# Attention into two mixtures on one core: 64-row score products, division after the value product, and first-mixture weight parts kept in DRAM

## The chip, the cores and the metric

One core of a Trainium2 chip runs the whole program. The metric is the device time of one execution in microseconds (us), the median of three runs for the kernel before. The profile is of one further execution. Engines are named as in the profile: PE (TensorE matmul), PEld (TensorE weight load), DVE (VectorE), ACT (ScalarE), POOL (GpSimd), SP (SyncE, which issues nearly all transfers).

## What is computed

```python
scores = scale * np.matmul(q, k.transpose(0, 1, 3, 2))     # 4 batches, 12 heads, 448 tokens, 64 wide
scores = np.where(mask, -1000000000.0, scores)             # causal
attn = np.exp(scores - np.max(scores, axis=-1, keepdims=True))
attn = attn / (np.sum(attn, axis=-1, keepdims=True) + 1e-09)
x = np.matmul(attn, v)                                     # then 1792 tokens x 768
h = np.maximum(np.maximum(x @ w1, x @ w2), x @ w3)         # first mixture, 768 x 768 each
y = h @ w_out
# second mixture: one of 8 experts per token, 768 -> 1024 -> 768, scaled by its gates
```

w1, w2, w3 and w_out arrive as 64-bit floats and are decoded on the chip; the rest is 32-bit.

## The kernel before, in words

The work goes in four batches of 448 tokens. A **unit** u is one pair of heads of one batch: units 0 to 5 are batch 0, 6 to 11 batch 1, up to 23. The two heads of a unit sit in partitions 0 to 63 and 64 to 127.

**First stage** (`first_heads`, an order written out by hand): attention of units 0 to 5, and the decoding of w_out and of three of the 18 chunks of w1 to w3. A chunk is 128 columns of one of the three matrices; the code cuts each matrix into six. The three chunks go to `wdram`.

**Middle stages** (`batch(b)`, b = 0, 1, 2; `mix`): `h_stream(b)` makes the hidden layer of batch b, chunk by chunk, and beside it the generator `attn_stream` computes the attention of batch b + 1, at 0.95 steps for each step of the host stream; `y_half` then multiplies by w_out for three or four blocks of 128 tokens, again with attention steps beside it. The order on each engine comes from a planner that sorts by priority; `ahead` runs with a higher one. **Batch 3** of `h_stream` runs without attention, beside the first loads of expert weights (`first_load`, 14 transfers). The second mixture follows, slot by slot.

Numbers on PE are carried as a high and a low part (float32r): a product is made of two or three matmuls. The steps around the change, per unit:

- `at_t` (L223): PE transposes q and k into PSUM. For units 0 to 9 (`NATQ`) they are copied as plain float32; from unit 10 on q and k are split: `qs` holds for each head the high part in its 64 partitions and the low part in the other 64, `ks` holds k's high part in both halves (written by L250 and copied across by L253), `kl` k's low part (L251).
- `at_qk` (L256): the scores of a head and of a block i of 112 queries against 112(i + 1) keys, so 112 to 448 columns. Units 0 to 9: one float32 product over 64 rows (L274). From unit 10: one product over 128 rows, high times high and low times high at once (L276), and one over 64 rows for k's low part (L278).
- `at_e` (L282): DVE adds the mask and finds the maximum (L292), ACT makes the exponential and the row sum (L297).
- `at_n` (L304): from unit 6 on, DVE adds 1e-9 to the sums (L308), takes the reciprocal (L309) and multiplies the four blocks of each head's probabilities by it (L315). For units 0 to 5 the probabilities are left as they are; `at_rb` and `at_r` spread the reciprocal over 64 columns (ACT, L320), transpose it (four PE transposes, L327) and copy it out (ACT), and `at_x` multiplies each head's finished value product by it (DVE, L398).
- `at_p` (L336): PE transposes the probabilities (L350), ACT and DVE split them (L361, L362). `at_av` (L365): the product with v; ACT moves the other half of the result across (L391) and DVE adds it into `xf` (L392).
- `x_split` (L450) splits `xf` for `h_stream`, once a unit is done.

The scores, transposes and value products share six PSUM banks (`ps_t`). From unit 12 on and in the first stage both heads' scores are made at once (six banks); for units 6 to 11 one head at a time (`at_s`).

The weights of the first mixture: `w_fetch` (L466) brings a chunk into `wr`. In batch 0 it is decoded from two raw halves (`decode_load` on SP, two ACT, three DVE and one POOL instruction each, L143 to L155) and written to `wdram` (L472); in batches 1 to 3 it is read back from there (L474). `w_split` (L477) then makes the high part on ACT (L482) and the low part on POOL (L483), in every batch. `ahead` keeps chunks fetched three to four ahead of use and split one to two ahead. SP issues in one order, so a fetch that waits for a free buffer holds back what is queued behind it.

```python
for a, (l, r) in enumerate(((wh, xh), (wh, xl), (wl, xh))):   # L515, six times a chunk
    nc.tensor.matmul(pm[:, :S], lhsT=l[:, kk, :], rhs=r, ...)
```

Of the kernel before, what the change touches and what calls it, by code (L numbers as in the profile page):

```python
# [32 lines left out]
def kernel(  # L33
# [221 lines left out]
    def at_qk(u, js):  # L255

        qs, ks, kl = qks[u]
        for i in range(NC):
# [3 lines left out]
            for j in js:  # L262
                m = M[j]
# [7 lines left out]
                sl.append((j, m, ss))  # L271
            for j, m, ss in sl:
                if u in NATQ:
                    nc.tensor.matmul(ss, lhsT=qs[m, 0, qc], rhs=ks[m, 0, :L], start=True, stop=True)  # L274
# [25 lines left out]
    def at_s(u, j, beside=()):  # L300
        at_qk(u, (j,))
        at_e(u, j, beside)

    def at_n(u, j):  # L304
        if u in NATP and j == 0:
            return
        sm = sums[u] if u in NATP else sums[u][:, j]
        nc.vector.tensor_scalar_add(sm, sm, 1e-9)  # L308
        nc.vector.reciprocal(sm, sm)  # L309
        if u in NATP:  # L310
            return
# [5 lines left out]
    def at_rb(u):  # L317
        rb = att.tile([P, 512], F32, tag="mn", name=f"rb{u}", bufs=1)[:CP].rearrange("p (c j d) -> p c j d", c=NC, j=2)
        sb = sums[u].rearrange("p j c -> p c j").unsqueeze(3).to_broadcast([CP, NC, 2, D])
        nc.scalar.copy(rb, sb)  # L320
# [851 lines left out]
```

## Time and profile before

| | |
|---|---|
| three runs | 1019.55, 1024.61, 1024.18 us; median 1024.18 |
| the profiled execution | 1027.47 us, span on the core 1025.8 us |
| PE, PEld busy in the span | 94%, 81% |
| DVE, ACT, POOL busy | 61%, 52%, 29% |
| mean granted clock of PE | 0.965 of full |
| moved by DMA | 122.95 MB, 120 GB/s in the mean |
| chain of waits, by engine | PE 65%, DVE 22%, ACT 5%, DMA 3% |

Times inside the profile are counted from the start of the span. The first matmul of `h_stream` starts at 99.4 us and its batches 1 to 3 at 287.1, 439.9 and 583.5; `y_half` of batch 2 ends at 594, `h_stream(3)` alone runs from there to 652.4, and the second mixture's slots run from about 704 to the end. Ends of matmuls are modelled, so a matmul's own row is longer than the time from its start to the next one's start.

### The profile page before, as it was taken

To read this page: it belongs to the slowest core of one execution; us is meant where nothing else is said; L and a number is where in the kernel's file an instruction comes from. 1 tells how busy PE (TensorE), PEld (TensorE's weight loads), DVE (VectorE), ACT (ScalarE), POOL (GpSimd) and SP (SyncE) were. 2 spreads that over 40 slices of the span, in tenths; PEclk is the share of its full clock that TensorE was granted. 3 is DMA by queue.
4 is the path that set the end of the run, shared out by engine and by line. 5 is a ranking of instruction groups with operands and counts; after the bars stand their busy time and mean duration, and the time that the engine had idled before them with its cause. 6 is when DMAs were issued, how large, how long until landed. Compare 5 with 4: busy or idle time off the path is not lost.

```text
span 1025.8 us, 16765 instructions
## 1 busy us (share of the span) xinstructions
PE 965.5 (94%) x5188; PEld 833.4 (81%) x5188; DVE 629.5 (61%) x1504; ACT 528.7 (52%) x1181; POOL 302.5 (29%) x249
## 2 busy tenths in 40 slices
PE   7998898888999999999998999988999999999997
PEld 4676676676887888897887989977989989898896
DVE  5887888999587877657788542292111114939344
ACT  7887564666565666545766223251212124838243
POOL 2445644544022335122444155132010100010101
PEclk9998987899998999998999999999999999999999
DMA  7566554642222333223312185036010112949600
GB/s 166 147 163 182 171 156 148 181 134 77 63 66 74 101 93 89 82 66 88 89 63 62 48 279 183 24 109 239 35 63 32 38 57 88 358 159 353 212 31 25
DMA packets 116418, 122.95 MB, mean 120 GB/s; under 512 B 74830, under 2 KB 92238, under 8 KB 116304
## 3 DMA queue, kind: packets, MB, share of 16 engines
q1 hardware_dynamic: 113264, 108.24, 34.1%
q0 software_dynamic: 3040, 13.41, 3.8%
q8 instruction: 44, 0.72, 0.3%
q14 instruction: 70, 0.57, 0.2%
HBM read 109.80 MB, written 19.69 MB: 126 GB/s over the span
## 4 chain that ended last, share of the span: by engine, by line
PE 65%; DVE 22%; ACT 5%; DMA 3%; issue 3%; SPq 1%; POOL 1%; DVEq 0%; POOLq 0%; ACTq 0%
PE pm L516 16%; PE po L1068 14%; PE ph L1049 14%; PE py L548 8%; DVE pt L315 5%; PE ss L276 2%; DVE ptl L362 2%; PE pp L350 2%; PE av L386 2%; PE ss L278 2%; ACT pt L297 2%; DMA xg<-ydram,gix 2%; DVE pt L292 2%; DVE dt L152 2%; PE pht L1060 1%
## 5 line engine op out<-in xcount | busy, mean ns | idle before, releaser
L483 POOL TENSOR_TENSOR wl<-wr,wh 128x768 fp32r<-128x768 f32 x72 | 134.6, 1869 | 206.5 <-ACT wh L482 186.6
L516 PE MATMUL pm<-xh,wh 128*128 128x448 f32 x432 | 169.7, 393 | 0.0
L516 PE MATMUL pm<-xh,wl 128*128 128x448 f32 x432 | 162.1, 375 | 1.0 <-POOL wl L483 1.0
L516 PE MATMUL pm<-xl,wh 128*128 128x448 f32 x432 | 162.3, 376 | 0.3 <-POOL xl L454 0.3
L297 ACT ACTIVATE pt<-pt,bm 112x112 f32<-112x112 f32 x192 | 100.7, 526 | 69.3 <-DVE bm L292 66.1
L1063 DVE TENSOR_TENSOR tl<-pht,th 128x512 fp32r<-128x512 f32 x36 | 24.8, 688 | 136.1 <-ACT th L1062 86.0
L1077 POOL DMA_INDIRECT out_dram<-os,six x18 | 18.4, 1020 | 283.5 <-ACT os L1076 171.4
L1068 PE MATMUL po<-w2h,th 128*128 128x384 f32 x288 | 100.7, 350 | 0.0
L1068 PE MATMUL po<-w2h,tl 128*128 128x384 f32 x288 | 97.6, 339 | 1.8 <-DVEq L1098 1.8
L1068 PE MATMUL po<-w2l,th 128*128 128x384 f32 x288 | 97.7, 339 | 0.0
L292 DVE CUSTOM_DVE_ANT_0 pt<-ss,mask 112x112 f32<-112x112 f32 x192 | 80.7, 441 | 25.0 <-PE ss L278 17.7
L482 ACT CAST wh<-wr 128x768 fp32r<-128x768 f32 x72 | 60.0, 834 | 69.2 <-PE pm L516 40.5
L516 PEld LDWEIGHTS pm<-xh,wh 128*128 128x128 f32 x432 | 84.1, 195 | 14.3 <-issue 6.9
L516 PEld LDWEIGHTS pm<-xh,wl 128*128 128x128 f32 x432 | 84.0, 194 | 9.2 <-POOL wl L483 1.7
L315 DVE TENSOR_SCALAR pt<-pt,sm 112x112 f32<-112x112 f32 (+3 forms) x144 | 88.6, 660 | 1.5
L516 PEld LDWEIGHTS pm<-xl,wh 128*128 128x128 f32 x432 | 84.4, 195 | 5.9 <-POOL xl L454 0.6
L1049 PE MATMUL ph<-w1l,xh 128*128 128x512 f32 x216 | 85.4, 396 | 2.6 <-DVE w1l L1038 2.6
L1049 PE MATMUL ph<-w1h,xh 128*128 128x512 f32 x216 | 86.4, 400 | 0.0
L1049 PE MATMUL ph<-w1h,xl 128*128 128x512 f32 x216 | 85.0, 393 | 0.0
L362 DVE TENSOR_TENSOR ptl<-pp,pth 112x448 fp32r<-112x448 f32 (+1 forms) x108 | 55.3, 538 | 20.1 <-ACT pth L361 19.6
L350 PE MATMUL pp<-ident,pt 112*112 112x112 f32 x480 | 62.8, 267 | 1.4 <-ACT pt L297 1.3
L350 PEld LDWEIGHTS pp<-ident,pt 112*112 112x112 f32 x480 | 54.8, 139 | 8.8 <-ACT pt L297 2.6
(232 smaller groups left out, 2071.5 us busy)
## 6 DMA issues: line engine op xcount, KB each, us to landing
wr<-wdram SPq DMA_DIRECT2D x57, 384.0 KB
w1r<-in_moe_w_dram SPq DMA_DIRECT2D x42, 512.0 KB
w2r<-in_moe_w_dram SPq DMA_DIRECT2D x56, 384.0 KB
raw<-in_moe_w_dram SPq DMA_DIRECT2D x36, 384.0 KB
wdram<-wr SPq DMA_DIRECT2D x15, 384.0 KB
qraw<-in_q_dram SPq DMA_DIRECT2D x48, 112.0 KB
kraw<-in_k_dram SPq DMA_DIRECT2D x48, 112.0 KB
vraw<-in_v_dram SPq DMA_DIRECT2D x48, 112.0 KB
```

The lines of the kernel that those rows point to most:

```text
L292: nc.vector.tensor_tensor_reduce(out=pr, in0=ss, in1=mask[:, S - L :], scale=1.0, scalar=3.0e38, op0=ALU.add, op1=ALU.min, accum_out=bm[:, ...
L297: nc.scalar.activation(pr, pr, AF.Exp, bias=bm[:, i : i + 1], scale=-1.0, accum_out=sm[:, j, i : i + 1])
L315: nc.vector.tensor_scalar_mul(pr, pr, sm[:, i : i + 1])
L350: nc.tensor.transpose(pp[:CP, off : off + CP], pt[:, POFF[i] + kt * CP : POFF[i] + (kt + 1) * CP], ident[:CP, :CP])
L362: nc.vector.tensor_sub(ptl[:, o0 : o0 + off], pp[:CP, :off], f32(pth[:, o0 : o0 + off]))
L482: nc.scalar.copy(wh, wr3)
L483: nc.gpsimd.tensor_sub(wl, wr3, f32(wh))
L516: nc.tensor.matmul(pm[:, :S], lhsT=l[:, kk, :], rhs=r, start=kk == 0 and a == 0, stop=kk == KD - 1 and a == 2)
L548: nc.tensor.matmul(pm[:, :w], lhsT=l[:, kk, cs], rhs=r[:, kk, c0 : c0 + w], start=kk == 0 and c == 0, stop=kk == KF - 1 and c == 2,)
L1049: nc.tensor.matmul(pm[a], lhsT=l[:, kk], rhs=r[kk][:, cs], start=kk == 0 and c == 0, stop=kk == KD - 1 and c == 2)
L1063: nc.vector.tensor_sub(tl[:, kr], pt, f32(th[:, kr]))
L1068: nc.tensor.matmul(po[a][:, :HN], lhsT=l[:, kk], rhs=r[kk][:, HN * a : HN * a + HN], start=kk == 0 and c == 0, stop=kk == KF2 - 1 and c == 2,)
```

## The change

Units 6 to 23 get the same form of attention: q and k are split into `qh`, `ql`, `kh`, `kl`, each 128 partitions with a head in each half, and the scores are three products over 64 rows per head (high high, low high, high low), the two heads in turn; both heads' scores are made at once in every unit. The probabilities are no longer multiplied; one reciprocal per unit is spread, transposed (`at_n`, `at_r`) and multiplied into `xf` after the second head's value product (`at_x`), read from PSUM.

In batch 0 both parts of each chunk are written to `wpdram` after the split (768 KB each, 18 times); in batches 1 to 3 both parts are read from there into one of three `wp` buffers, and no split is made. The decoded chunks of batch 0 past the first three are no longer written. Buffers `wraw` and `wt` move to another pool.

```diff
-    NATQ = range(10)
-    NATP = range(6)
+    NAT = range(6)
...
+    wdram = dram.tile([ND, P, KD * P], F32, name="wdram")
+    wpdram = dram.tile([3 * KF, P, 2 * KD * P], F32, name="wpdram")
...
     def at_t(u):
...
+            qh, ql, kh, kl = (att.tile([P, S], F32R, tag=t, name=f"{t}{u}", bufs=1) for t in ("qh", "ql", "kh", "kl"))
...
-        for j in range(2 if u not in NATQ else 0):
-            nc.scalar.activation(qs[M[j], j], pq[M[j], :S], AF.Copy, scale=-SCALE)
+        nc.scalar.activation(qh, pq[:, :S], AF.Copy, scale=-SCALE)
+        if ql is not None:
             nc.vector.scalar_tensor_tensor(
-                out=qs[O[j], j], in0=pq[M[j], :S], scalar=-SCALE, in1=f32(qs[M[j], j]), op0=ALU.mult, op1=ALU.subtract
+                out=ql, in0=pq[:, :S], scalar=-SCALE, in1=f32(qh), op0=ALU.mult, op1=ALU.subtract
             )
...
-        for j in range(2):
-            nc.scalar.copy(ks[M[j], j], pk[M[j], :S])
-            nc.vector.tensor_sub(kl[M[j]], pk[M[j], :S], f32(ks[M[j], j]))
-        for j in range(2):
-            nc.vector.tensor_copy(ks[O[j], j], f32(ks[M[j], j]))
+        nc.scalar.copy(kh, pk[:, :S])
+        nc.vector.tensor_sub(kl, pk[:, :S], f32(kh))
...
+        prods = ((qh, kh),) if u in NAT else ((qh, kh), (ql, kh), (qh, kl))
...
-                    nc.tensor.matmul(ss, lhsT=qs[:, j, qc], rhs=ks[:, j, :L], start=True, stop=False)
-            for j, m, ss in sl if u not in NATQ else ():
-                nc.tensor.matmul(ss, lhsT=qs[m, j, qc], rhs=kl[m, :L], start=False, stop=True)
+            for n, (l, r) in enumerate(prods):
+                for m, ss in sl:
+                    nc.tensor.matmul(ss, lhsT=l[m, qc], rhs=r[m, :L], start=n == 0, stop=n == len(prods) - 1)
...
-        pt = heads[u, j]
-        for i in range(NC):
-            pr = pt[:, POFF[i] : POFF[i] + CP * (i + 1)]
-            nc.vector.tensor_scalar_mul(pr, pr, sm[:, i : i + 1])
...
+    def at_n(u):
+
+        nc.vector.tensor_scalar_add(sums[u], sums[u], 1e-9)
+        nc.vector.reciprocal(sums[u], sums[u])
+        rb = att.tile([CP, NC, 2, D], F32, tag="rb", name=f"rb{u}", bufs=1)
+        nc.scalar.copy(rb, sums[u].rearrange("p j c -> p c j").unsqueeze(3).to_broadcast([CP, NC, 2, D]))
...
+        rs[u] = pr
+        if u in NAT:
+            rs[u] = att.tile([P, S], F32, tag="rs", name=f"rs{u}", bufs=1)
+            nc.scalar.copy(rs[u], pr[:, :S])
...
+        if j is None:
+            nc.vector.tensor_mul(x, rs[u][:, :S], x)
...
     def attn_stream():
...
+            if last:
+                at_qk(u)
                 at_e(u, 0)
...
-            at_n(u, 0)
-            if u >= 2 * NP:
-                at_e(u, 1)
-            else:
-                at_s(u, 1)
+            at_e(u, 1)
             yield
-            if u > NP:
+            if last:
                 at_av(u - 1, 1)
+                at_r(u - 1)
+                at_x(u - 1)
                 done.add(u - 1)
...
+            at_n(u)
...
     def w_fetch(b, i):
+        if b:
+            wp = wst.tile([P, 2, KD, P], F32R, tag="wp", name=f"wp{b}_{i}", bufs=WB)
+            nc.sync.dma_start(out=f32(wp).rearrange("p a k n -> p (a k n)"), in_=wpdram[i])
+            wtiles[b, i] = (wp[:, 0], wp[:, 1])
+            return
...
-            nc.sync.dma_start(out=wdram[wi, f], in_=wr)
...
     def w_split(b, i):
+        if b:
+            return
...
+        nc.scalar.copy(wp[:, 0], wr3)
+        nc.gpsimd.tensor_sub(wp[:, 1], wr3, f32(wp[:, 0]))
+        nc.sync.dma_start(out=wpdram[i], in_=f32(wp).rearrange("p a k n -> p (a k n)"))
...
-            ahead(n, AHEAD, SPLIT)
+            ahead(n, AHEAD if b == 0 else WB - 1, SPLIT)
...
-                    ahead(n, AHEAD + 1, SPLIT + 1)
+                    ahead(n, AHEAD + 1 if b == 0 else WB, SPLIT + 1)
...
     def first_heads():
...
-        at_s(NP, 0)
+        at_qk(NP)
+        at_e(NP, 0)
```

## Rows read from the trace of the kernel before

**Rows 1.** Busy time by stage: h_stream(0) with y, (1), (2), then (3) alone.

```profile
core 0: us, PE busy (x) PEld busy (x) DVE busy (x) ACT busy (x) POOL busy (x), PEclk, DMA share, GB/s
99.40:287.10 187.70, 166.56 (x802) 135.75 (x802) 157.05 (x358) 111.80 (x280) 81.78 (x67) 0.89 0.44 131
287.10:439.90 152.80, 145.57 (x830) 127.52 (x831) 116.22 (x285) 93.99 (x233) 51.84 (x39) 0.98 0.31 86
439.90:594.10 154.20, 145.97 (x820) 127.93 (x820) 113.05 (x329) 85.23 (x210) 50.01 (x44) 0.97 0.24 71
594.10:652.40 58.30, 58.30 (x290) 54.07 (x289) 16.50 (x18) 17.33 (x25) 28.83 (x16) 1.00 0.57 196
```

**Rows 2.** The chain of waits by line, in the first three of these stages.

```profile
by line: DVE pt L315 15.2%; PE py L548 9.6%; PE pm L516 8.3%; issue 6.2%; DVE dt L152 5.2%; DVE ptl L362 5.1%; DVE dt L151 4.9%; ACT pt L297 4.3%; PE ss L274 4.3%; DVE dt L150 4.1%; DVE htl L534 3.3%; PE pp L350 2.5%; PE av L386 2.4%; PE ss
...
by line: PE pm L516 27.2%; PE py L548 13.8%; DVE pt L315 9.4%; PE ss L276 7.5%; PE ss L278 5.4%; PE av L386 4.8%; PE pp L350 4.5%; DVE ptl L362 4.4%; DVE qs L240 3.3%; DVE ks L253 3.1%; DVE kl L251 2.6%; issue 2.4%; DVE g L528 1.9%; ACT pt 
...
by line: PE pm L516 31.2%; PE py L548 9.1%; DVE pt L315 8.1%; PE ss L276 5.9%; PE pp L350 5.8%; PE av L386 5.1%; PE ss L278 4.4%; DVE ptl L362 3.7%; issue 2.5%; DVE qs L240 2.4%; ACT pt L297 2.1%; DVE ks L253 2.0%; DVE htl L534 2.0%; DVE g 
```

**Rows 3.** Groups of instructions, whole span: count, busy us, mean ns, idle before.

```profile
L315 DVE TENSOR_SCALAR pt<-pt,sm 112x112 f32<-112x112 f32 (+3 forms) x144 | 88.6, 660 | 1.5
...
L240 DVE SCALAR_TENSOR_TENSOR qs<-pq,qs 64x448 fp32r<-64x448 f32 x28 | 17.4, 622 | 0.9
...
L251 DVE TENSOR_TENSOR kl<-pk,ks 64x448 fp32r<-64x448 f32 x28 | 17.4, 622 | 0.7
...
L253 DVE CAST ks<-ks 64x448 fp32r<-64x448 f32 x28 | 14.0, 501 | 0.7
...
L398 DVE TENSOR_TENSOR xf<-av,rs 64x448 f32<-64x448 f32 x12 | 7.5, 622 | 6.3 <-ACT rs L331 4.1 <-PE av L374 2.0
...
L482 ACT CAST wh<-wr 128x768 fp32r<-128x768 f32 x72 | 60.0, 834 | 69.2 <-PE pm L516 40.5 <-issue 18.1 <-POOL wl L483 9.5
...
L483 POOL TENSOR_TENSOR wl<-wr,wh 128x768 fp32r<-128x768 f32 x72 | 134.6, 1869 | 206.5 <-ACT wh L482 186.6 <-PE pp L350 19.8
...
L320 ACT COPY rb<-sm 112x512 f32<-112x512 f32 x6 | 3.7, 618 | 0.8 <-ACT qk L237 0.4 <-DVE sm L309 0.3
...
L327 PE MATMUL pr<-ident,rb 112*128 112x112 f32 x24 | 3.3, 259 | 0.0
```

**Rows 4.** PE in order of time, the scores of one unit of batch 2.

```profile
297.93 0.44 PE L276 MATMUL ss<-ks,qs 128*112 128x112 f32 x2
298.30 0.31 PE L278 MATMUL ss<-kl,qs 64*112 64x112 f32 x2
298.53 0.46 PE L276 MATMUL ss<-ks,qs 128*112 128x224 f32 x2
...
300.63 0.46 PE L278 MATMUL ss<-kl,qs 64*112 64x448 f32 x2
301.01 0.47 PE L516 MATMUL pm<-xh,wh 128*128 128x448 f32 x1
```

**Rows 5.** Matmuls and weight loads of `h_stream` in order of time.

```profile
224.03 0.37 PE L516 MATMUL pm<-xl,wh 128*128 128x448 f32 x1
224.04 0.19 PEld L516 LDWEIGHTS pm<-xh,wl 128*128 128x128 f32 x1
224.24 0.36 PE L516 MATMUL pm<-xh,wl 128*128 128x448 f32 x1
```

**Rows 6.** The chain: float32 scores of one unit of 6 to 9.

```profile
129.18 4.00 PE ss L274 x8
```

**Rows 7.** Busy time of shorter stretches: y alone, two with dense transfers, and that of rows 6.

```profile
420.00:440.00 20.00, 20.00 (x120) 19.88 (x119) 9.47 (x29) 8.66 (x24) 2.71 (x3) 1.00 0.19 61
600.00:620.00 20.00, 20.00 (x100) 18.55 (x99) 6.16 (x7) 5.94 (x9) 9.77 (x6) 1.00 0.94 322
940.00:960.00 20.00, 20.00 (x111) 18.13 (x110) 15.97 (x22) 13.66 (x21) 1.99 (x2) 1.00 0.99 364
129.20:133.10 3.90, 3.90 (x8) 1.95 (x8) 3.02 (x10) 2.27 (x9) 1.99 (x2) 0.50 0.70 177
```

More of the change, by code (lines that the diff above doesn't have):

```diff
@@ L261, in at_qk @@
             sl = []
-            for j in js:
-                m = M[j]
+            for j in range(2):
                 if i < 2:
@@ L270, in at_qk @@
                     ss = scs[u, j][-1][:CP, :L]
[L271 to L274, printed above, removed]
-                else:
-                    nc.tensor.matmul(ss, lhsT=qs[:, j, qc], rhs=ks[:, j, :L], start=True, stop=False)
-            for j, m, ss in sl if u not in NATQ else ():
-                nc.tensor.matmul(ss, lhsT=qs[m, j, qc], rhs=kl[m, :L], start=False, stop=True)
+                sl.append((M[j], ss))
+            for n, (l, r) in enumerate(prods):
+                for m, ss in sl:
+                    nc.tensor.matmul(ss, lhsT=l[m, qc], rhs=r[m, :L], start=n == 0, stop=n == len(prods) - 1)
     def at_e(u, j, beside=()):
@@ L298, in at_e @@
         heads[u, j] = pt
[L300 to L311, printed above, removed]
-        pt = heads[u, j]
-        for i in range(NC):
-            pr = pt[:, POFF[i] : POFF[i] + CP * (i + 1)]
-            nc.vector.tensor_scalar_mul(pr, pr, sm[:, i : i + 1])
[L317 to L320, printed above, removed]
+    def at_n(u):
[3 more added lines that the diff above has]
+        nc.scalar.copy(rb, sums[u].rearrange("p j c -> p c j").unsqueeze(3).to_broadcast([CP, NC, 2, D]))
         rs[u] = rb
@@ L329, in at_r @@
             )
-        rs[u] = att.tile([P, S], F32, tag="rs", name=f"rs{u}", bufs=1)
-        nc.scalar.copy(rs[u], pr[:, :S])
+        rs[u] = pr
+        if u in NAT:
+            rs[u] = att.tile([P, S], F32, tag="rs", name=f"rs{u}", bufs=1)
+            nc.scalar.copy(rs[u], pr[:, :S])
     pts, rs, avs = {}, {}, {}
@@ L394, in at_av, with at_x @@
             del vss[u]
[L396 to L398 removed]
+    def at_x(u, j=None):
+        x = xf[u % NP]
+        if j is None:
+            nc.vector.tensor_mul(x, rs[u][:, :S], x)
+        else:
+            nc.vector.tensor_mul(x[M[j]], avs.pop((u, j))[M[j], :S], rs[u][M[j]])
     done = set()
@@ L441, in attn_stream @@
             yield
-        at_n(NU - 1, 1)
-        at_p(NU - 1, 1, PB[0])
-        at_p(NU - 1, 1, PB[1])
+        u = NU - 1
+        at_p(u, 1, PB[0])
+        at_p(u, 1, PB[1])
         yield
-        at_av(NU - 1, 1)
-        done.add(NU - 1)
+        at_av(u, 1)
+        at_r(u)
+        at_x(u)
+        done.add(u)
         yield
@@ L466, in w_fetch @@
     def w_fetch(b, i):
-        f, wi = divmod(i, 3)
-        wr = wst.tile([P, KD * P], F32, tag="wraw", name=f"wr{b}_{i}")
-        if b == 0 and i >= ND:
+        if b:
[3 more added lines that the diff above has]
+            return
+        wr = dec.tile([P, KD * P], F32, tag="wraw", name=f"wr{b}_{i}", bufs=3)
+        if i >= ND:
             for a in range(2):
                 decode(wr[:, HC * a : HC * (a + 1)], decode_load(w_src(i, a)))
-            nc.sync.dma_start(out=wdram[wi, f], in_=wr)
         else:
-            nc.sync.dma_start(out=wr, in_=wdram[wi, f])
+            nc.sync.dma_start(out=wr, in_=wdram[i])
         wtiles[b, i] = wr
     def w_split(b, i):
+        if b:
+            return
         wr = wtiles[b, i]
-        wh = wst.tile([P, KD, P], F32R, tag="wh", name=f"wh{b}_{i}", bufs=2)
-        wl = wst.tile([P, KD, P], F32R, tag="wl", name=f"wl{b}_{i}", bufs=2)
+        wp = wst.tile([P, 2, KD, P], F32R, tag="wp", name=f"wp{b}_{i}", bufs=WB)
         wr3 = wr.rearrange("p (k n) -> p k n", k=KD)
-        nc.scalar.copy(wh, wr3)
-        nc.gpsimd.tensor_sub(wl, wr3, f32(wh))
-        wtiles[b, i] = (wh, wl)
+        nc.scalar.copy(wp[:, 0], wr3)
+        nc.gpsimd.tensor_sub(wp[:, 1], wr3, f32(wp[:, 0]))
+        nc.sync.dma_start(out=wpdram[i], in_=f32(wp).rearrange("p a k n -> p (a k n)"))
+        wtiles[b, i] = (wp[:, 0], wp[:, 1])
     seq = [(b, i) for b in range(B) for i in range(NCH)]
@@ L630, in first_heads @@
             if u % 2:
-                f, wi = divmod(u // 2, 3)
-                nc.sync.dma_start(out=wdram[wi, f], in_=cw)
+                nc.sync.dma_start(out=wdram[u // 2], in_=cw)
             if u < NP - 1:
```

60 lines of the change are left out of this document (22 added, 38 removed).

## The prediction

> **What bounds the kernel now.** I read busy times by stage first [rows 1], then the chain of waits in the same stages [rows 2], because the means over the span mix a first mixture with attention beside it and a second one without.
>
> [...] DVE works 157.1 of the 187.7 us [rows 1]. On the chain the largest entry is DVE's multiplication of the probabilities (L315), 15.2% or 28.5 us, and the three DVE steps of the decoding (L150 to L152) have 14.2%, 26.7 us [rows 2]. This stage is bound by DVE, with decoding and normalising in one queue.
>
> In the stages of batches 1 and 2 PE idles only 7.2 and 8.2 us, the clock is 0.98 and 0.97, and the chain is led by PE's own matmuls (L516, L548); DVE's L315 follows with 9.4% and 8.1%, 14.4 and 12.5 us [rows 1, 2]. They are nearly bound by PE. In batch 3 alone PE has no gap in 58.3 us [rows 1]. What follows is not touched.
>
> **The change, part by part.**
>
> *DVE.* A unit had eight multiplications of 660 ns in the mean over 144, but their busy time is 88.6 us, so 88.6/18 = 4.9 us a unit for units 6 to 23 [rows 3]. They go. From unit 10 on, q's and k's low parts take one instruction each over 128 partitions instead of two over 64: 2 x 0.62 us saved, if 128 partitions cost what 64 do; and the two copies L253 go, 1.0 us. One multiplication of `xf` comes, 0.62 us by L398 [rows 3]. The sums are treated once a unit instead of twice; I leave that small gain out. So a unit from 10 on loses 4.9 + 1.2 + 1.0 - 0.6 = 6.5 us, and one of 6 to 9, whose two low parts are new against one copy (about +0.6), 3.7 us. In all 14 x 6.5 + 4 x 3.7 = 106 us of DVE out of the 386 us that it works in the three stages. By units (6 to mid 12; mid 12 to 18; 19 to 23) that is about 31, 42 and 33 us.
>
> *PE, scores.* From unit 10 on a unit's scores now take 301.01 - 297.93 = 3.08 us [rows 4]. The columns alone would be far less; each pass from 128-row to 64-row matmuls and back shows a pause. A 64-row pair holds PE for 298.53 - 298.30 = 0.23 us at 112 columns and 301.01 - 300.63 = 0.38 us at 448, and its two matmuls go together: 336 columns more add 0.15 us, which is one matmul's stream, not two [rows 4]. After the change there are three such pairs for each of four blocks. If every pair pays the single price (0.23, 0.28, 0.33, 0.38 by interpolation) that is 3 x 1.22 = 3.66 us. If the weight loads go beside the pair before, as they do in `h_stream`, where a load starts 0.01 us after the matmul ahead of it and the next matmul follows 0.2 us after the last for 448 columns [rows 5], the pairs cost about 0.10, 0.11, 0.15 and 0.20 us, 1.7 us in all and some 0.3 for entering and leaving: 2.0 us. I take 2.0, since rows 5 show the overlap within one set of rows, and keep both ends: -1.1 or +0.6 us a unit.
>
> [...]
>
> Units 6 to 9 have float32 scores of 4.00 us at a clock of 0.50, so 2.0 us at full clock [rows 6, 7]: no change at the lower end, +1.7 at the upper.
>
> *PE, the reciprocal.* Four transposes a unit: 3.3/24 x 4 = 0.55 us [rows 3]. They wait for ACT's spreading copy (0.62 us, L320), which is emitted a full unit earlier; PE's queue behind them holds `h_stream`. For the last unit of a batch the chain grows by them and by 0.62 us of DVE before its split, 1.2 us at most, inside the y blocks. So PE: -1.1 + 0.55 = -0.55 us from unit 10 on, +0.55 for 6 to 9.
>
> *ACT and POOL.* 54 splits go: 54 x 0.83 = 45 us of ACT and 54 x 1.87 = 101 us of POOL [rows 3]. Neither is on the chain with more than a trace [rows 2], so I cost it at nothing; the work that hides them is PE's, and at worst nothing is gained. ACT gets 18 copies of 0.62 us and loses about one us a unit in `at_t`.
>
> *Transfers.* Batch 0 writes 18 x 768 instead of 15 x 384 KB, 8.3 MB more; batches 1 to 3 read 7.1 MB more each. SP waits for POOL's split before each write, with raw halves for the decoding and q, k, v queued behind; a fetch of parts waits until PE is done with the chunk three earlier, with q, k, v, the results of y and, in batch 3, the expert weights behind it. In the stage of batch 0 the share of the engines is 0.44 at 131 GB/s; at the densest, 364 GB/s at 0.99 [rows 1, 7]. 8.3 MB cost 22 us of share: (0.44 x 187.7 + 22)/160 = 0.65 of a stage of 160 us. Not a bound in the mean. In batches 1 and 2, 7.1 MB on 71 to 86 GB/s leave it below 0.5. In batch 3 chunks take 58.3 us at 196 GB/s; 15 fetches more than double in size add 5.9 MB: 297 GB/s in the mean, under 364. But in the first 20 us, where the expert weights go, 322 GB/s at 0.94 become (6.4 + 2.2)/0.02 = 430: 23.6 us of transfers in 20. Two chunks are in store. I take +3 us, ends 0 and +12.
>
> **The sum.** Batch 0 stage: what L315 has on the chain, 28.5, less 3 for transposes: the decoding is late next, and stays. So -25, ends -8 (decoding takes its place at once) and -42 (idle and half of the 41 us at the lower clock both come back). Batch 1 stage: idle 7.2, and the lower clock costs 0.02 x 152.8 = 3.1; the stretch of y with DVE at 9.5 of 20 us has no gap at all [rows 7], and DVE falls to 74 of some 139 us here, so all returns, and 6.5 x 0.55 = 3.6 from PE: -14, ends -3 and -24 (all of L315, the copies and half of L240 and L251 on the chain). Batch 2 stage: half of the idle 8.2, since the routing's own steps stand at its end (an estimate), 0.03 x 154.2 = 4.6 for the clock, and 5 x 0.55 = 2.8: -12, ends -3 and -20. Batch 3 +3. First stage: the second head's scores of unit 6 only move forward, 0, ends -1 and +2.
>
> Sum -48. The profiled execution took 1027.47 us, span and 1.7 around it; 1027.47 - 48 = 979.5, and the median of the runs stands 0.3% lower: **977 us**.
>
> **Rivals.**
>
> *Scores by the single price.* Each of 14 units loses 1.7 us more, each of 4 likewise: +30, so 1007. For: the pauses between the kinds of matmuls [rows 4]. Against: rows 5. Chance 0.12. [...]
>
> *PE was the bound and DVE its cover.* In batches 1 and 2 "idle" is so little that DVE's relief gives nothing, and in batch 0 the decoding steps in: -10, -4, -3: about 1005. For: the chain's lead of L516 and L548 [rows 2]. Against: the idle and the low clock in batch 0. Chance 0.12.
>
> *The decoding starves.* In batch 0 raw halves queue on SP behind writes that wait for POOL, and each write is twice as long; the gain there falls to 5: 997. For: DMA's larger share. Against: 0.65 is not full. Chance 0.12.
>
> *Slower: parts come late in batch 3.* With 768 KB a chunk and two expert loads in between, a chunk's fetch lands after PE wants it; PE stops in each chunk and its clock falls to the lower level, where rows 7 show matmuls at half pace (0.50). Whole batch: 58.3 us become 117, so 977 - 3 + 58 = 1032. A chunk takes PE 18 x 0.205 = 3.7 us [rows 5]; this decides once all 18 take 2.5 us longer, so once parts come at under 0.79 MB/6.2 us = 127 GB/s. By the sums above only the first seven come near, with 364 less the expert loads' share. Chance 0.06.
>
> That the change does not do what it says has no room: the instructions are in the diff.
>
> **How the numbers follow.** Forecast 0.58, its own range 950 to 1000; the others as given. The range 948 to 1013 takes in the forecast's bounds, the three rivals at 997 to 1007, and leaves out the slower one and the extremes where all ends meet (937 and 1024). A measurement of this kernel can tell about 0.5%, 5 us: I count one in ten of the four faster cases, 0.94 together, as lost to what is not in them, most of it to no change: faster than 1019 with 0.85, within with 0.06, slower with 0.09.
>
> **What would show it.** Right: L315 and L253 gone, no split in batches 1 to 3; the stages at about 163, 139 and 142 us; a clock near 1.00 in all; scores of a unit near 2.0 us in PE's order of time; PE without gaps in batch 3, or some 3 us of them in its first 25 us. Wrong: the decoding's DVE steps with the chain share that L315 had, and a stage of batch 0 above 180 us; scores near 3.7 us; waits of PE for `wp` with the clock at 0.50.

## The result, and the profile after

The changed kernel takes 983.11 us (median of 4 runs, 980.61 to 984.32) where the kernel before, beside it on the same chip, takes 1022.97: a ratio of 0.961, interval 0.958 to 0.965. Two later measurements, on two chips, put it at 981.9 and 982.1 us with the kernel before at 1028.4 and 1028.3 (ratios 0.955 and 0.957, below). So some 40 to 46 us are gained. The profiled execution is the shortest of its runs, 980.61 us with a span of 978.8; that of the kernel before was the longest of its own. Differences of stages are of these two executions, so differences of under about 2 us are not leaned on.

One border ahead of the prediction was read wrong: `y` of batch 2 ends at 583.3, not 594, and the first matmul of `h_stream(3)` starts at 583.5. What began at 594.1 was only the stretch in which PE runs without a break. These are the two last stages of the kernel before by the right border (windows of stages; us, busy time of each engine with instructions, granted clock, DMA share, GB/s):

```profile
439.90:583.50 143.60, 136.71 (x771) 120.58 (x770) 103.18 (x278) 83.35 (x206) 48.14 (x43) 0.96 0.24 71
583.50:652.40 68.90, 67.56 (x339) 61.42 (x339) 26.38 (x70) 19.22 (x29) 30.70 (x17) 1.00 0.52 175
```

And the same view of the changed kernel: the first stage, then the stages of batches 0 to 3, each from its first matmul of `h_stream` to that of the next:

```profile
0.00:102.30 102.30, 89.14 (x538) 64.92 (x538) 74.94 (x235) 81.53 (x223) 41.42 (x46) 0.93 0.66 176
102.30:270.00 167.70, 146.98 (x866) 130.10 (x866) 126.75 (x283) 109.46 (x273) 77.01 (x66) 0.92 0.60 188
270.00:407.90 137.90, 137.37 (x904) 126.61 (x903) 71.17 (x202) 76.64 (x208) 17.95 (x21) 1.00 0.49 146
407.90:535.90 128.00, 128.00 (x834) 117.67 (x833) 70.16 (x213) 66.65 (x183) 14.23 (x25) 1.00 0.42 135
535.90:604.50 68.60, 68.33 (x340) 61.50 (x340) 18.45 (x70) 6.66 (x13) 1.13 (x1) 1.00 0.75 274
```

Against [rows 1] and the two lines above: batch 0 from 187.7 to 167.7 us, batch 1 from 152.8 to 137.9, batch 2 from 143.6 to 128.0, batch 3 from 68.9 to 68.6; the first stage grew from 99.4 to 102.3, and what follows stayed (373.4 and 374.3). In batches 1 and 2 PE now stands idle for 0.5 and 0 us, at a clock of 1.00; DVE fell from 116 and 103 us to 71 and 70, POOL from 52 and 48 to 18 and 14. In batch 0 PE still stands idle for 20.7 us, where it was 21.1, and the clock is 0.92: what fell there is PE's busy time, from 166.6 to 147.0 us. The chain of waits of batch 1's stage, which had L315 with 9.4% and five more DVE lines [rows 2], is all but PE alone:

```profile
by line: PE pm L501 46.6%; PE py L533 18.9%; PE av L364 10.1%; PE ss L269 8.1%; PE pp L328 7.8%; PE pr L303 1.7%; PE pq L235 1.7%; PE pk L243 1.7%; issue 0.0%
```

The scores of one unit of batch 2, in PE's order of time, the counterpart of [rows 4]:

```profile
281.28 0.31 PE L269 MATMUL ss<-kh,qh 64*112 64x112 f32 x2
281.38 0.18 PEld L269 LDWEIGHTS ss<-kh,ql 64*112 64x112 f32 x2
281.43 0.26 PE L269 MATMUL ss<-kh,ql 64*112 64x112 f32 x2
281.47 0.18 PEld L269 LDWEIGHTS ss<-kl,qh 64*112 64x112 f32 x2
281.52 0.26 PE L269 MATMUL ss<-kl,qh 64*112 64x112 f32 x2
...
282.45 0.36 PE L269 MATMUL ss<-kh,qh 64*112 64x448 f32 x2
282.65 0.36 PE L269 MATMUL ss<-kh,ql 64*112 64x448 f32 x2
282.85 0.37 PE L269 MATMUL ss<-kl,qh 64*112 64x448 f32 x2
...
283.15 0.47 PE L501 MATMUL pm<-xh,wp 128*128 128x448 f32 x1
```

Pairs follow one another after 0.15, 0.09 and, at 448 columns, 0.20 us, which is also the distance of two full-height matmuls of 448 columns [rows 5]; so the load of the next pair's weights, on the same rows, falls into the time of the pair ahead of it (it starts at 281.38 and 281.47, 0.10 and 0.04 us after that pair). The unit takes 283.15 - 281.28 = 1.87 us; it is 1.86 or 1.87 in each of the eleven units of the stages of batches 1 and 2. In the kernel before these eleven took 2.96 to 7.54 us, and only those without a wait in them some 3 as in [rows 4]; in all they took 47.1 us and take 20.5 now, 26.6 less, where the two stages are 30.5 us shorter.

Groups of the whole span that answer to [rows 3]: the splits of weights are 18 instead of 72, the transposes of the reciprocals 96 instead of 24, and a low part of q or k is one instruction over 128 partitions at the price of one over 64 (623 ns against 622).

```profile
L467 POOL TENSOR_TENSOR wp<-wr,wp 128x768 fp32r<-128x768 f32 x18 | 33.3, 1851 | 21.0 <-ACT wp L466 14.3 <-issue 4.8 <-DMA raw<-in_moe_w_dram 1.7
...
L303 PE MATMUL pr<-ident,rb 112*128 112x112 f32 x96 | 13.6, 265 | 0.9 <-ACT rb L296 0.9
L377 DVE TENSOR_TENSOR xf<-pr,xf 128x448 f32<-128x448 f32 x18 | 11.2, 625 | 1.7
L238 DVE SCALAR_TENSOR_TENSOR ql<-pq,qh 128x448 fp32r<-128x448 f32 x18 | 11.2, 623 | 3.9 <-ACT qh L236 3.6
```

### The profile page after: what moved, and what is told of

Its sections match the earlier page's. It is cut to its first block, busy times and chain, and to the rows that moved or that the text cites. A ratio compares the mean times of both kernels' runs of the same rounds, so it can differ in the third digit from the quotient of the medians.

```text
span 978.8 us, 16842 instructions
## 1 busy us (share of the span) xinstructions
PE 931.1 (95%) x5404; PEld 827.9 (85%) x5404; DVE 513.7 (52%) x1290; ACT 482.8 (49%) x1121; POOL 199.6 (20%) x195
## 4 chain that ended last, share of the span: by engine, by line
PE 69%; DMA 2%; DVE 0%; ACT 0%; issue 0%; POOL 0%; POOLq 0%; ACTq 0%
PE pm L501 20%; PE po L1052 15%; PE ph L1033 14%; PE py L533 7%; PE av L364 3%; PE pp L328 2%; PE ss L269 2%; DMA xg<-ydram,gix 2%; PE pht L1044 2%; PE pxt L975 1%; PE pr L303 0%; PE pk L243 0%; PE pq L235 0%; ACT w1h L1021 0%; PE pmt L834 0%
## 5 line engine op out<-in xcount | busy, mean ns | idle before, releaser
L501 PE MATMUL pm<-xh,wp 128*128 128x448 f32 x864 | 277.1, 384 | 2.8 <-POOL wp L467 2.8
L501 PEld LDWEIGHTS pm<-xh,wp 128*128 128x128 f32 x864 | 166.9, 194 | 21.8 <-issue 4.7
L501 PE MATMUL pm<-xl,wp 128*128 128x448 f32 x432 | 161.8, 375 | 0.5 <-POOL xl L433 0.5
L288 ACT ACTIVATE pt<-pt,bm 112x112 f32<-112x112 f32 (+1 forms) x192 | 100.4, 524 | 46.7 <-DVE bm L283 45.0
L1052 PE MATMUL po<-w2h,tl 128*128 128x384 f32 x288 | 97.4, 338 | 1.7 <-DVEq L1082 1.7
L1052 PE MATMUL po<-w2l,th 128*128 128x384 f32 x288 | 97.4, 338 | 0.0
L283 DVE CUSTOM_DVE_ANT_0 pt<-ss,mask 112x112 f32<-112x112 f32 (+1 forms) x192 | 79.4, 443 | 20.4 <-PE ss L269 11.7
L501 PEld LDWEIGHTS pm<-xl,wp 128*128 128x128 f32 x432 | 84.2, 195 | 6.6 <-POOL xl L433 0.9
L339 ACT CAST pth<-pp 112x448 fp32r<-112x448 f32 (+1 forms) x108 | 47.4, 472 | 42.4 <-PE pp L328 42.3
L513 DVE TENSOR_TENSOR g<-pm,g 128x448 f32<-128x448 f32 x48 | 29.9, 622 | 56.4 <-PE pm L501 56.0
L533 PE MATMUL py<-woh,hth 128*128 128x400 f32 (+1 forms) x168 | 59.3, 353 | 0.0
L533 PE MATMUL py<-woh,htl 128*128 128x400 f32 (+1 forms) x168 | 57.5, 342 | 0.0
```

Source lines behind the costliest of these rows:

```text
L283: nc.vector.tensor_tensor_reduce(out=pr, in0=ss, in1=mask[:, S - L :], scale=1.0, scalar=3.0e38, op0=ALU.add, op1=ALU.min, accum_out=bm[:, ...
L288: nc.scalar.activation(pr, pr, AF.Exp, bias=bm[:, i : i + 1], scale=-1.0, accum_out=sm[:, j, i : i + 1])
L339: nc.scalar.copy(pth[:, o0 : o0 + off], pp[:CP, :off])
L501: nc.tensor.matmul(pm[:, :S], lhsT=l[:, kk, :], rhs=r, start=kk == 0 and a == 0, stop=kk == KD - 1 and a == 2)
L513: nc.vector.tensor_max(g, pm[:, :S], g)
L533: nc.tensor.matmul(pm[:, :w], lhsT=l[:, kk, cs], rhs=r[:, kk, c0 : c0 + w], start=kk == 0 and c == 0, stop=kk == KF - 1 and c == 2,)
```

## The experiments

The change has three parts that can be had alone: (a) the division behind v, (b) the scores as 64-row products, (c) the parts of the weights in DRAM. All kernels below have their stages in the table at the end of this section.

**Without (c).** Chunks are fetched whole and split in every batch, as before; the larger writes of batch 0 go, and the buffers of the chunks move back:

```diff
     def w_fetch(b, i):
-        if b:
-            wp = wst.tile([P, 2, KD, P], F32R, tag="wp", name=f"wp{b}_{i}", bufs=WB)
-            nc.sync.dma_start(out=f32(wp).rearrange("p a k n -> p (a k n)"), in_=wpdram[i])
...
     def w_split(b, i):
-        if b:
-            return
...
```

> The changed kernel with the weights of the first mixture handled as before: one 384 KB copy per chunk in DRAM, split again on ACT and POOL in every batch. My theory: these splits lay beside PE's work, so the time stays within 4 us of the changed kernel's 983 us and PE still has no gaps in batches 1 and 2. Rival one, the parts carry a share of the gain (POOL and DVE get in each other's way, or PE waits for a split): 990 to 1000 us. Rival two, the larger transfers cost something in batch 0: 972 to 979 us, with the batch 0 stage under 160 us.

Measured 991.42 us, ratio 0.965 [0.961, 0.969], 9.3 us above the changed kernel on the same chip (982.13, below), where at most 4 were expected. But little of it lies where the splits are. Of the 54 splits that come back, 52 fall in the stages of batches 1 to 3. Those of batches 1 and 2 here:

```profile
278.50:416.40 137.90, 137.36 (x904) 126.47 (x903) 76.87 (x202) 89.59 (x226) 51.46 (x39) 1.00 0.35 95
416.40:546.30 129.90, 128.79 (x835) 117.67 (x833) 77.79 (x214) 79.51 (x201) 47.72 (x43) 1.00 0.27 79
```

Batch 1 takes what it takes in the changed kernel, batch 2 is 1.9 us longer and batch 3 about one. The first stage (106.4 us against 102.3 to 102.5 in three executions of the changed kernel) and batch 0 (172.1 against 167.7 to 169.6) show 6 to 8 us together, and they have 2 splits as there and 18 instead of 16. What makes them longer, the other writes or the buffers, no run tells.

What the splits do to DVE is plain all the same. The low part of the hidden layer in batches 1 and 3 (36 in all; these 12 have 448 columns), in the groups of the kernel before:

```profile
L534 DVE TENSOR_TENSOR htl<-g,hth 128x448 fp32r<-128x448 f32 x12 | 15.5, 1293 | 3.6 <-ACT hth L533 3.5
```

of the changed kernel:

```profile
L519 DVE TENSOR_TENSOR htl<-g,hth 128x448 fp32r<-128x448 f32 x12 | 7.8, 648 | 4.4 <-ACT hth L518 4.4
```

and of this one, where POOL splits again:

```profile
L512 DVE TENSOR_TENSOR htl<-g,hth 128x448 fp32r<-128x448 f32 x12 | 19.0, 1584 | 4.7 <-ACT hth L511 4.6
...
L461 POOL TENSOR_TENSOR wl<-wr,wh 128x768 fp32r<-128x768 f32 x72 | 134.0, 1861 | 191.6 <-ACT wh L460 138.9 <-PE ss L268 19.8 <-PE pp L327 15.2
```

These means mix two kinds. In this kernel eleven of the twelve run beside a POOL instruction, in 880 to 1903 ns, and one alone, in 626; in the changed kernel eleven run alone, in 615 to 627, and one beside POOL, in 931. One of each, in order of time, first of this kernel, then of the changed one:

```profile
594.30 1.86 POOL L461 TENSOR_TENSOR wl<-wr,wh 128x768 fp32r<-128x768 f32 x1 [1.79 <-ACT wh L460]
594.80 1.83 DVE L512 TENSOR_TENSOR htl<-g,hth 128x448 fp32r<-128x448 f32 x1 [0.63 <-ACT hth L511]
...
594.79 0.63 DVE L519 TENSOR_TENSOR htl<-g,hth 128x448 fp32r<-128x448 f32 x1 [0.63 <-ACT hth L518]
```

The subtractions with one operand in PSUM are not held: 59 of these 108 run beside a POOL instruction, and none takes more than 625 ns (least, median and most, this kernel):

```profile
L339 DVE TENSOR_TENSOR ptl<-pp,pth x108: 374/614/625, 111.9 to 531.5; 112x448 fp32r<-112x448 f32 x72, 112x224 fp32r<-112x224 f32 x36
```

In the kernel before the order of time shows the same for the four multiplications of one head, 4.40 us where 4 x 0.66 would be 2.6:

```profile
185.02 4.40 DVE L315 TENSOR_SCALAR pt<-pt,sm 112x112 f32<-112x112 f32 x4
185.81 1.83 POOL L483 TENSOR_TENSOR wl<-wr,wh 128x768 fp32r<-128x768 f32 x1
187.65 1.53 POOL L220 TENSOR_TENSOR vs<-vraw,vs 112x256 fp32r<-112x256 f32 x2
```

The subtraction at 594.80 ends at 596.63, 0.47 us after the split beside it, and takes 0.63 us where POOL has none beside it. What makes it wait is not shown.

So in these runs a split holds up such subtractions (1.83 us for 0.63) and multiplications (4.40 us for 2.6) of DVE beside it, and what that costs hangs on whether something waits for DVE: with (a) and (b) in place (c) takes nothing from batch 1, with (a) alone 4 us (table). ACT's splits go and come with POOL's in all these runs, so the two are not told apart there.

**Without (a).** The multiplications come back ahead of each head's `at_p`, and the transposes and the product on `xf` go:

```diff
+    def at_m(u, j):
+        sm = sums[u][:, j]
+        nc.vector.tensor_scalar_add(sm, sm, 1e-9)
+        nc.vector.reciprocal(sm, sm)
+        pt = heads[u, j]
+        for i in range(NC):
+            pr = pt[:, POFF[i] : POFF[i] + CP * (i + 1)]
+            nc.vector.tensor_scalar_mul(pr, pr, sm[:, i : i + 1])
...
-                at_r(u - 1)
-                at_x(u - 1)
...
-            at_n(u)
...
```

> The changed kernel with the probabilities multiplied by the reciprocal again in units 6 to 23, and no reciprocal behind the value product. My theory: this is the largest part; the batch 0 stage goes from 168 to about 190 us, batches 1 and 2 gain 1 to 3 us each since DVE has room there now: 1008 us, 1003 to 1015. Rival, that the scores carry most and the multiplications are hidden once the scores are shorter: under 995 us.

Measured 976.05 us, some 6 below the changed kernel: the expectation falls, with its sign, and the rival's time came (under 995 us). Because this decides what (a) is worth, both kernels were measured again, five times each on one chip:

> The changed kernel beside the next one on one chip. Theory: the division behind the value product costs PE four transposes in each of 18 units and gives nothing back where PE sets the pace: this one is 4 to 8 us slower than the next, its stages of batches 1 and 2 at 138 and 128 us. Rival, that the two stood on different chips: within 2 us of each other.

> The run with the probabilities multiplied by the reciprocal, again: 4 to 8 us under the changed kernel on the same chip, batches 1 and 2 at 136 and 126 us.

Measured 982.13 us (979.89 to 983.18) and 976.58 us (975.52 to 979.28). Without the division behind v the kernel is 5.5 us faster. Its stages of batches 1 and 2:

```profile
271.60:408.00 136.40, 135.73 (x877) 123.83 (x877) 92.58 (x261) 73.36 (x203) 18.73 (x21) 1.00 0.51 148
408.00:533.90 125.90, 125.90 (x811) 115.37 (x810) 81.76 (x258) 64.14 (x178) 14.83 (x25) 1.00 0.44 137
```

The changed kernel in the same comparison has 137.90 and 128.00 us again, with the busy times shown above to 0.05 us. DVE has 21 and 12 us more to do here, and PE still stands idle for only 0.7 and 0 us. PE has 27 and 23 matmuls fewer, and the stages are 1.5 and 2.1 us shorter. Of the 5.5 us these two stages show 3.6. The rest can't be placed: the two profiled executions, 979.28 and 979.89 us, are the slowest and the fastest of their kernels and differ by 0.6 us in all.

**Without (b).** The stacked scores of before, both heads of a unit at once; one buffer of y less, so that it fits:

```diff
...
+    NATQ = range(10)
...
+            for j, m, ss in sl:
+                if u in NATQ:
+                    nc.tensor.matmul(ss, lhsT=qs[m, 0, qc], rhs=ks[m, 0, :L], start=True, stop=True)
+                else:
+                    nc.tensor.matmul(ss, lhsT=qs[:, j, qc], rhs=ks[:, j, :L], start=True, stop=False)
+            for j, m, ss in sl if u not in NATQ else ():
+                nc.tensor.matmul(ss, lhsT=qs[m, j, qc], rhs=kl[m, :L], start=False, stop=True)
```

> The changed kernel with q and k of units 10 to 23 stacked as before (a 128-row and a 64-row product), units 6 to 9 with float32 scores, and one buffer less for y so that it fits. My theory: PE takes 3.0 us instead of 1.86 for the scores of 14 units, 16 us, in stages where PE sets the pace, and 1 to 2 us are won in batch 0: 997 us, 992 to 1002. Rival one, the shorter scores only removed DVE copies that were hidden: within 4 us of 983. Rival two, the copies of k stall PE as in the kernel before, where single units took 4 to 7.5 us: over 1005 us.

Measured 992.98 us, 11 above the changed kernel, near what was expected. A unit's scores take 2.96 us, and the stages of batches 1 and 2 are 6.0 and 4.9 us longer: 6 and 5 units of 1.1 us, less 0.6 and 0.6. Batch 0 is 8 to 10 us longer, where 1 to 2 less were expected, and the first stage 5 us shorter.

**(a) alone**: the two edits without (b) and without (c) together.

> The kernel before with the division behind the value product alone: scores stacked, weights split in every batch, both heads' scores at once. If the parts add, it stands where the two runs above stand together above the changed kernel: about 997 us. If the removed multiplications were the whole gain: 983 to 988. If they were a cover for PE's own time: over 1010.

Measured 1008.33 us, ratio 0.982 [0.978, 0.985]: 20 us gained, 11 less than the 31 that were expected. By what the two runs above measured, 9.3 and 10.9 us over the changed kernel, it would stand at 1002.3: the parts don't add. The same subtraction takes 1504 ns in the mean here, as without (c).

The changed kernel, in the comparison of these:

> The changed kernel once more, on the chip of the next three. If the run with the multiplications was faster for a reason of its own and not by the chip, this one stands at 0.96 of the kernel before and its stages of batches 1 and 2 again 1.4 and 2.3 us above those of that run.

Measured 981.9 us, ratio 0.955 [0.952, 0.958].

**None of the three**: what is left of the edit is that both heads' scores of units 6 to 11 come at once.

> The kernel before with one thing of the change alone: both heads' scores of units 6 to 11 at once, as was done from unit 12 on. In all runs so far it was in. Theory: it gives little in itself, 1019 to 1028 us where before has 1028, and batch 0 ends near 285 us. Rival, it is what shortened the stage of batch 0 in all of them: 1010 to 1016 us, batch 0 ending near 280 us as with the division alone.

Measured 1029.96 us, ratio 1.003 [1.001, 1.004]: the order alone gives nothing. Its stage of batch 0 is the one to compare the others with:

```profile
98.10:284.90 186.80, 156.74 (x800) 132.23 (x800) 155.80 (x348) 110.56 (x273) 82.79 (x67) 0.89 0.44 130
```

PE is busy for 9.8 us less than in the kernel before and stands idle for 30.1 us instead of 21.1.

**What still holds batch 0.** While the last weights are decoded PE waits; afterwards it hardly does (windows of the changed kernel; the last decoding step on DVE ends at 208.8):

```profile
102.30:206.00 103.70, 83.91 (x437) 71.79 (x437) 86.68 (x173) 67.39 (x158) 59.41 (x50) 0.87 0.71 225
206.00:270.00 64.00, 63.07 (x430) 58.31 (x430) 40.07 (x111) 42.08 (x116) 17.61 (x16) 0.99 0.42 128
```

Its largest waits in the first of the two (engine, line, releaser, us, times, longest):

```profile
PE av L364 <- DVE ptl L340: 7.3, 6, 2.5
PE pp L328 <- DVE bm L283: 6.9, 4, 2.4
```

A third buffer for raw halves, on the kernel without (a):

```diff
-        raw = dec.tile([P, HC, 2], I32, tag="raw", name="raw")
+        raw = dec.tile([P, HC, 2], I32, tag="raw", name="raw", bufs=3)
...
-        wt = dec.tile([P, KD, P], F32, tag="wt", name=f"wt{f}", bufs=1)
+        wt = dec.tile([P, KD, P], F32, tag="raw", name=f"wt{f}", bufs=3)
```

> The run with the probabilities multiplied, and three buffers instead of two for the raw halves of the decoding (the first stage's transposed w_out shares them). My new theory: batch 0 is paced by the decoding, one half in about 3.9 us in all kernels so far, since with two buffers a raw half's transfer and its decoding alternate; with a third the halves come in 3.2 us or less and the batch 0 stage falls from 167 to 145 to 155 us: 955 to 966 us. Rival, DVE's queue is the limit (141 of 167 us busy): the halves stay at 3.7 to 3.9 us and the time at 973 to 978.

Measured 981.31 us, no less than the changed kernel on the same chip (981.9) and 5 more than the same kernel without the third buffer on another. The last decoding step on DVE ends about 6 us earlier (208.4 against 213.9 and 214.7 in two executions without it), and yet the stage of batch 0 is 172.8 us long where it was 167.2 and 169.7. Neither the theory nor its rival came: the decoding is earlier and the stage is no shorter.

No division at all in units 6 to 23 (the three calls of `at_m` gone):

```diff
-                at_m(u - 1, 1)
...
-            at_m(u, 0)
...
-        at_m(u, 1)
```

> Leaves out the division for units 6 to 23 altogether: no multiplication, no reciprocal, no transposes. Read by stages up to the end of batch 3, as the routing may differ. My theory: PE paces batches 1 and 2, so they take what they took with the multiplications, 136 and 126 us, within 1 us; batch 0, paced by the decoding, 160 to 167. Rival, DVE still matters: batches 1 and 2 under 133 and 123, batch 0 under 155.

Measured 973.52 us in a single run, which leaves the division out, so that its numbers are not those of the program. With (b) and (c) in place the multiplications and reciprocals cost about 3 us in all (976.58 with them, on another chip), 1.3 and 0.4 of it in batches 1 and 2.

One DVE step of decoding less, on the changed kernel (the clamp is left out):

```diff
-        yield nc.vector.tensor_scalar(out=t, in0=t, scalar1=LO, scalar2=HI, op0=ALU.max, op1=ALU.min)
```

> The changed kernel, leaving out the clamp of the decoding (L151, 0.58 us on DVE for each of 48 halves). If each half's own chain paces batch 0 and two buffers share it, 30 halves are shorter by 0.3 us each or a little more: the batch 0 stage falls from 168 to 156 to 160 us. If DVE's queue is the limit, by the whole 17 us: to 151. If neither, it stays within 3 us.

Measured 976.7 us in a single run. The stage of batch 0 is 169.3 us, as long as in the changed kernel (167.7 to 169.6), so neither the halves' own chain nor DVE's queue of decoding steps alone paces it; what is gained lies in the first stage (98.0).

**A version that beats both**: the kernel without (a), with the float32 scores of before in units 6 to 9.

```diff
+    NATQ = range(10)
...
-        if u in NAT:
+        if u in NATQ:
...
-        prods = ((qh, kh),) if u in NAT else ((qh, kh), (ql, kh), (qh, kl))
+        prods = ((qh, kh),) if u in NATQ else ((qh, kh), (ql, kh), (qh, kl))
```

> The run with the probabilities multiplied, and float32 scores for units 6 to 9: one copy each of q and k instead of two parts, 2.08 us of PE instead of 1.86. Theory: up to the end of batch 0 PE waits for other engines, so the split of these units costs more there than the matmuls; the first stage ends at 97 to 99 us instead of 103 and batch 0 at 264 to 268 instead of 270: 970 to 974 us where the run before it has 976. Rival, the waits move elsewhere: within 2 us of it.

Measured 974.43 us (972.58 to 975.26), ratio 0.948 [0.947, 0.950]: 7.7 us under the changed kernel on the same chip, 2.2 under the one without (a). By stages it is the first (98.1 us against 101.9) and batch 0 (166.9 against 169.7), as expected.

The lengths of the stages, each from its first matmul of `h_stream` to the next one's, the time that PE stands idle in the stage of batch 0, and the median (a single run for no division and no clamp; before and changed of the first comparison on top):

| kernel | first | batch 0 | idle in 0 | 1 | 2 | 3 | after | median us |
|---|---|---|---|---|---|---|---|---|
| before | 99.4 | 187.7 | 21.1 | 152.8 | 143.6 | 68.9 | 373.4 | 1022.97 |
| changed, (a) + (b) + (c) | 102.3 | 167.7 | 20.7 | 137.9 | 128.0 | 68.6 | 374.3 | 983.11 |
| none, both heads at once | 98.1 | 186.8 | 30.1 | 154.5 | 142.3 | 69.0 | 375.0 | 1029.96 |
| (a) | 99.1 | 181.5 | 27.0 | 147.8 | 138.4 | 69.0 | 374.8 | 1008.33 |
| (a) + (b) | 106.4 | 172.1 | 24.9 | 137.9 | 129.9 | 69.0 | 375.3 | 991.42 |
| (a) + (c) | 97.4 | 177.6 | 23.2 | 143.8 | 133.0 | 68.2 | 373.2 | 992.98 |
| (b) + (c) | 101.9 | 169.7 | 23.6 | 136.4 | 125.9 | 68.8 | 374.8 | 976.58 |
| (b) + (c), third raw buffer | 101.6 | 172.8 | 22.9 | 136.4 | 125.9 | 68.3 | 374.7 | 981.31 |
| (b) + (c), no division | 102.6 | 165.9 | 23.2 | 135.1 | 125.5 | 68.9 | 373.9 | 973.52 |
| changed, no clamp | 98.0 | 169.3 | 24.7 | 137.8 | 128.1 | 68.8 | 372.9 | 976.70 |
| (b) + (c), float32 in 6 to 9 | 98.1 | 166.9 | 16.4 | 136.4 | 125.9 | 68.8 | 375.5 | 974.43 |

On the chips of all rows but the first two the kernel before has a median of 1028.3 or 1028.4 us.

## Why the prediction was right, and where its reasons were not

The forecast of 977 us is 6 us, 0.6%, under the first measurement and 5 under the later ones; the sum of -48 us stands against -47.0 between the two spans, -46 between the medians of 15 and 5 runs (1028.3 and 982.1) and -40 between those of the first measurement. That the sum is so near is luck in part: batch 0 gave 5 us less than its term and the first stage lost 3, while batches 2 and 3 did better by 4 and 3. Each term:

- **Batch 0, -25, measured -20.0.** The size was nearly right and the reason failed. The step was that the stage gets back "what L315 has on the chain, 28.5, less 3 for transposes". Putting the multiplications back into the changed kernel costs this stage nothing that can be told: 167.2 and 169.7 us in two executions against 167.7, 168.4 and 169.6. PE's idle time grows by some 3 us (24.7 and 23.6 against 20.6 to 21.2), and its busy time falls by 1 to 6 (142.5 and 146.1 against 147.0 to 148.4), since the transposes go. Against none of the three parts (186.8), (a) alone takes 5 us from it, (a) and (c) 9, (a) and (b) 15 while the first stage grows by 8. (b) takes it mostly from PE's busy time, 154.4 us in (a) + (c) and 147.0 with (b) as well; (a) and (c) take it mostly from the idle time (table). The end of -42 counted half of 41 us at a lower clock, a term that no row or run shows as such; in windows of 1 us this stage of the kernel before has 38 at a granted clock of 0.50, 143 at 1.00 and 7 between, that of the changed kernel 20, 134 and 14. That L315 stood on the chain because DVE was full there, and that the parts move one and the same wait, fits these numbers but is argued and not shown. "The decoding is late next, and stays" held: PE idles 19.8 us of the 103.7 us of decoding, at a clock of 0.87, where a clock near 1.00 had been forecast for all stages.
- **Batches 1 and 2, -14 and -12, measured -14.9 and -15.6.** PE all but without a gap and at a clock of 1.00, as forecast: the idle time went from 7.2 and 6.9 us to 0.5 and 0 and the clock from 0.98 and 0.96 to 1.00, where PE no longer waits for DVE. The instruction that it waited for was not L315 but the copy of k's high part, 6.1 of 7.2 us of idle time in batch 1 and 4.0 of 6.9 in batch 2 (kernel before: us, times, longest; then the longest of batch 1 in order of time):

```profile
PE ss L276 <- DVE ks L253: 6.1, 4, 2.5
PE ss L276 <- DVE ks L253: 4.0, 3, 2.5
...
319.78 1.80 POOL L483 TENSOR_TENSOR wl<-wr,wh 128x768 fp32r<-128x768 f32 x1 [4.83 <-ACT wh L482]
320.65 1.18 DVE L253 CAST ks<-ks 64x448 fp32r<-64x448 f32 x1
321.98 0.40 PE L276 MATMUL ss<-ks,qs 128*112 128x112 f32 x1 [2.49 <-DVE ks L253]
```

  (b) has no such copy. With (a) alone these waits fall from 6.2 and 3.4 us (none of the three) to 2.0 and 1.9, and with (a) and (c) to nothing though the copy is there. After the longest of them the clock is 0.50 from 322 to 328.5 us, and that unit's scores take the 7.54 us, the wait of 2.49 in them. So each part shortens or removes the same wait, which is why they don't add here: (b) and (c) without (a) leave PE idle for 0.7 and 0 us.
- **Border of batch 2.** The 142 us forecast for batch 2 were counted to the wrong border, 10.5 us late, and by the right one 131.6 were forecast and 128.0 came.
- **Scores, 2.0 us a unit, measured 1.87.** Taking the overlap from [rows 5] was right: at 448 columns pairs on the same rows follow one another after 0.20 us, and the rival at the single price (3.66 us, 1007) is out. For units 6 to 9 [rows 6] was misread: its 4.00 us are one head, and `at_s` makes the two one after the other (unit 7):

```profile
129.10 4.07 PE L274 MATMUL ss<-qk 64*112 64x112 f32 x8
139.97 2.14 PE L274 MATMUL ss<-qk 64*112 64x112 f32 x8
```

  The first of these ran at a granted clock of 0.50, the second at 1.00, with 2.07 us from its start to the next matmul's. So such a unit had some 4.1 us of scores at full clock (an estimate, twice 2.07) and not 2.0, and "no change" left out about 2 us of PE a unit, in a stage where PE does not set the pace alone.
- **Transposes, 0.55 us a unit, measured 0.32.** The busy time is as forecast, 13.6/24 = 0.57, but it counts rows that overlap; from the start of the four to the next matmul PE gives them 0.32 us in batches 1 and 2:

```profile
290.86 0.55 PE L303 MATMUL pr<-ident,rb 112*128 112x112 f32 x4
291.18 0.45 PE L501 MATMUL pm<-xh,wp 128*128 128x448 f32 x1
```

  By that, 27 and 23 transposes are 2.2 and 1.8 us, and the stages are 1.5 and 2.1 us shorter without them: they are what (a) costs where PE sets the pace. That DVE's relief by (a) pays for them there failed, since (b) and (c) have already relieved it.
- **Splits of ACT and POOL, cost "at nothing".** This term was mis-sized. (c) as a whole is worth 9.3 us in the change ((a) + (b) against all three) and 15.3 with the stacked scores ((a) against (a) + (c)). Batches 1 to 3, where the splits went, show 2 to 3 us of the first; of the second, batches 1 and 2 show 9.4. The prediction asked whether POOL was on the chain and not what POOL does to DVE; the mean of 660 ns for L315 already had it inside, and the longest wait above stands behind a copy L253 of 1.18 us beside a split, where its median is 0.39. With 18 splits the same multiplications take 513 ns:

```profile
L298 DVE TENSOR_SCALAR pt<-pt,sm 112x112 f32<-112x112 f32 (+3 forms) x144 | 67.3, 513 | 1.5
```

- **Batch 3, +3, measured -0.3.** The parts come in time: 274 GB/s at a share of 0.75 in the mean, and PE busy 68.33 of 68.6 us. The rival that is slower found no place.
- **First stage, 0 with ends -1 and +2, measured +2.9.** Unit 6's scores stop in the middle: in the changed kernel ACT's copy of the reciprocals stands behind a split that waits for its chunk from DRAM, and PE behind that copy (order of time; idle before and releaser in brackets):

```profile
90.85 0.83 ACT L466 CAST wp<-wr 128x768 fp32r<-128x768 f32 x1 [0.91 <-DMA wr<-wdram]
91.58 0.53 ACT L309 COPY rs<-pr 128x448 f32<-128x448 f32 x1
92.16 0.43 PE L269 MATMUL ss<-kh,qh 64*112 64x112 f32 x1 [2.72 <-ACT rs L309]
...
96.01 4.15 PE L352 MATMUL av<-pth,vraw 112*128 112x448 f32 x8 [0.43 <-DVE bm L283]
```

and late in that wait the clock falls to 0.50, from 91 to 101 us (0.62 in the mean of the stretch below); pairs of scores at 448 columns follow one another after 0.37 us there instead of 0.20, and the `av` at 96.01 takes 4.15 us where one at 84.56 took 2.19:

```profile
88.00:99.50 11.50, 8.35 (x44) 6.16 (x43) 8.13 (x27) 8.90 (x27) 4.19 (x3) 0.62 0.91 273
```

  In the version that beats both PE waits 0.66 us for that copy, and the clock of 88 to 98 us is 0.97.

The rivals "PE was the bound and DVE its cover" and "the decoding starves" gave about 1005 us (1007 by its own terms) and 997 us and both are out as totals, though the second names the place where most is left: 19.8 us of idle PE.

Not settled: what paces PE in batch 0 while decoding goes on. The multiplications, a third raw buffer, one DVE step of decoding and the larger writes were each taken away or added without the stage getting shorter by more than 2 us against the changed kernel (165.9 at best). The waits shown are round trips of attention through DVE (`bm`, `ptl`); that these alone hold it is argued and not shown. Open too is what (c) changes in the first stage and in batch 0.

## What to carry to other kernels

POOL had 1% of the chain of waits in the kernel before, and yet a DVE subtraction of 626 ns took up to 1903 beside it: before costing work on POOL at nothing, compare the same DVE instruction with and without POOL beside it, and then ask whether anything waits for DVE in that stage. Two parts that relieved the same engine did not add here, so a part has to be taken out of the finished change to see what it is worth there; the division behind v gave 20 us alone and cost 5.5 us in the company of the other two. The chain says what waits, and only an edit says what that wait is worth.
